# Score tiles in runs of six, whole turns and hashes, whole v products, and three two-bank score buffers

One NeuronCore of one Trainium2 chip. The metric is the device time of one execution in microseconds, the median over several runs; lower is better.

## The reference

Hash attention feeds a feed-forward block. Queries and keys get a six-bit hash; a query sees only keys of its own bucket. The result goes through two matrices with a PReLU between.

```python
batch, n_heads, seq, head_dim = (4, 8, 768, 64)          # proj: (64, 6)
q_bucket, k_bucket = ...                                  # sign bits of q @ proj, k @ proj
scores = np.where(q_bucket == k_bucket, q @ k.T / 8, -1e9)
x = softmax(scores) @ v                                   # -> (3072, 512)
h = x @ w_in                                              # w_in (512, 2048)
g = np.maximum(h, 0) + alpha * np.minimum(h, 0)
out = g @ w_out                                           # w_out (2048, 512)
```

## The kernel before

Heads are worked on in 16 pairs, each in two units of 384 queries. For a unit there are six score tiles (128 keys by two heads by 384 queries), each a bf16 hash product plus a float32 product in one two-bank buffer of PSUM (the memory in which this kernel's TensorE products land; it uses eight banks of it), followed by one exp on ScalarE (ACT). A "turn" is the transposition of q or k. Probabilities are multiplied with v on TensorE (PE) and added up on VectorE (DVE), one addition being done by an accumulating DMA. Meanwhile DVE prepares the feed-forward weights, so that each feed-forward block needs seven products instead of eight. Each block has three accumulators in PSUM, called a, b and c. Early in the feed-forward a "verdict" is reached: a check of the largest magnitudes, which says whether the result of this fast way may stand.

```python
psum = tc.tile_pool(name="ps", bufs=2, space=PSUM)        # tags sc (2 banks each), mi, av: 8 banks

def turn(pi, name, half):            # 3 transposes into one "mi" bank, one ACT copy
def hash_bits(pi, half):             # 4 matmuls into one "mi" bank, three ACT signs
def scores(u, part):                 # two score tiles
    for kc in (2 * part, 2 * part + 1):
        sc = psum.tile([P, 2, 512], F32, tag="sc")
        ...                          # 4 matmuls, then exp on ACT into pt
def attend(u, half): ...             # v product over 3 key tiles into "av"
def totals(u): ...                   # sum over keys into "mi"

class Product:                       # one feed-forward block
    def times(self, bank, left, right, start):
        if start:
            tag, shape = {"a": ("sc", [P, 2, 512]), "b": ("mi", [P, 512]), "c": ("av", [P, 512])}[bank]
            t = psum.tile(shape, F32, name=f"{self.name}{bank}", tag=tag)
            self.ps[bank] = (t[:, 0] if bank == "a" else t)[:, : self.width]
        ...
    # 1: a, ACT copies a; 2: b; 22: DVE adds b; 5: c, ACT copies c; 6: a, ACT copies a;
    # 3: c, DVE adds c; 7: a, ACT copies a; 4 (after step 1 of the next block): a

for u in range(UNITS):               # shortened: order of the TensorE work
    scores(u, 0)
    turn(pi + 1, "q", ...) or hash_bits(pi + 1, 0)
    attend(u - 1, 0)
    scores(u, 1)
    attend(u - 1, 1); totals(u - 1)
    scores(u, 2)
    turn(pi + 1, "k", ...) or hash_bits(pi + 1, 1)
```

## Time and profile before

| | before |
|---|---|
| time, median of the 3 runs (range) | 975.83 us (975.73 to 978.42) |
| PE busy, share of the span | 98% |
| attention, first score to first product b of the feed-forward | 12.7 to 386.0 us |
| feed-forward, from there to the end | 386 to 973 us |
| one pair of heads in attention | 23.15 us |
| one feed-forward block, first matrix / second matrix | 9.03 / 24.17 us |

A row of waits is: who waited <- for whom: us in total, times, longest. A row of busy time is: stretch, length, then busy time of PE, weight loads, DVE, ACT and POOL with counts, granted clock of PE (1.00 is full speed), DMA share, GB/s. A timeline row is: start, length, engine, source line, operation, tiles written and read, part of the array in use with shape and type, count, and in brackets the idle time before it with what ended it.

### The profile page before, as it was taken

The numbers are of one execution on the slowest core, as the hardware profiler recorded it, in microseconds if no ns is written. First come the engines' busy times: TensorE is split into PE (matmuls) and PEld (weight loads), VectorE is DVE, ScalarE is ACT, GpSimd is POOL, SyncE is SP. The second block draws the span as 40 slices with busy tenths as digits, with TensorE's granted clock in tenths as the row PEclk, the third lists the DMA queues.
The fourth block names the chain that finished last, engine by engine and source line by source line (L and its number), as shares of the span: only waits on it lengthen the run. The fifth ranks groups of instructions, "written<-read, shape, count | busy, mean of one in ns | idle before, by whom it ended". The sixth has DMA issues, their size and how long they took to land.

```text
span 973.3 us, 12433 instructions
## 1 busy us (share of the span) xinstructions
PE 953.9 (98%) x4741; PEld 589.9 (61%) x4741; DVE 552.9 (57%) x995; ACT 371.5 (38%) x669; POOL 64.8 (7%) x62
## 2 busy tenths in 40 slices
PE   6999999999999999999999999999999999999997
PEld 3444444444444444556888556888556888556885
DVE  3788888898998887765400665301666301666000
ACT  6777776777777773222000222001222001222000
POOL 1000110000000010000300000200001200000000
PEclk9999999999999999999999999999999999999999
DMA  8767879699777643844100234100234100221000
GB/s 208 166 157 174 217 175 291 164 224 225 193 198 193 161 125 88 347 190 140 49 23 33 76 113 143 47 24 31 76 114 154 47 22 22 87 103 38 22 22 25
DMA packets 102020, 119.40 MB, mean 123 GB/s; under 512 B 53808, under 2 KB 88640, under 8 KB 101952
## 3 DMA queue, kind: packets, MB, share of 16 engines
q1 hardware_dynamic: 91680, 105.54, 34.7%
q0 software_dynamic: 8704, 12.58, 7.6%
q8 instruction: 39, 0.64, 0.3%
q10 hardware_dynamic: 1568, 0.39, 0.2%
q14 instruction: 29, 0.24, 0.1%
HBM read 78.65 MB, written 27.26 MB: 109 GB/s over the span
## 4 chain that ended last, share of the span: by engine, by line
PE 97%; ACT 1%; DVE 1%; DMA 0%; issue 0%; SPq 0%; ACTq 0%; DVEq 0%
PE sc L668 16%; PE av L703 14%; PE z_2a L773 6%; PE z_1a L773 6%; PE z_0a L773 6%; PE z_2c L773 3%; PE z_1c L773 3%; PE z_0c L773 3%; PE hs L651 2%; PE f_0a L773 2%; PE sm L715 2%; PE f_2a L773 2%; PE f_3a L773 2%; PE f_7a L773 2%; PE f_6a L773 2%; PE f_5a L773 2%
## 5 line engine op out<-in xcount | busy, mean ns | idle before, releaser
L673 ACT ACTIVATE pt<-sc 128x768 f32<-128x768 f32 x192 | 150.3, 813 | 97.4 <-PE sc L668 92.6
L668 PE MATMUL sc<-qT,kT 64*128 64x384 f32 x768 | 155.2, 482 | 0.0
L703 PE MATMUL av<-pt,vn 128*64 128x385 f32 (+1 forms) x768 | 138.1, 495 | 0.0
L703 PEld LDWEIGHTS av<-pt,vn 128*64 128x64 f32 x768 | 49.4, 136 | 76.7 <-issue 76.7
L827 DVE TENSOR_TENSOR g<-g,g 128x384 f32<-128x384 f32 x128 | 84.0, 677 | 2.2
L668 PEld LDWEIGHTS sc<-qT,kT 64*128 64x128 f32 x768 | 68.7, 189 | 21.0 <-issue 20.9
L668 PE MATMUL sc<-qb,kb 64*128 64x384 bf16 x384 | 63.6, 328 | 2.7 <-ACT pt L673 2.6
L685 POOL DMA_DIRECT2D accp<-pt x32 | 38.5, 1204 | 335.0 <-ACT pt L673 161.3
L668 PEld LDWEIGHTS <-kb 64*128 64x128 bf16 x384 | 19.1, 93 | 66.1 <-issue 52.3
L773 PE MATMUL z_2a<-wo,g 128*128 128x256 f32 x256 | 58.0, 379 | 0.5 <-ACT z_2u L780 0.5
L773 PE MATMUL z_0a<-wo,g 128*128 128x256 f32 x256 | 57.9, 379 | 0.0
L773 PE MATMUL z_1a<-wo,g 128*128 128x256 f32 x256 | 57.9, 379 | 0.0
L773 PEld LDWEIGHTS z_2a<-wo,g 128*128 128x128 f32 x256 | 48.6, 190 | 8.1 <-ACT z_2u L780 0.9
L773 PEld LDWEIGHTS z_0a<-wo,g 128*128 128x128 f32 x256 | 48.6, 190 | 7.5
L773 PEld LDWEIGHTS z_1a<-wo,g 128*128 128x128 f32 x256 | 48.6, 190 | 6.6
L820 DVE SCALAR_TENSOR_TENSOR g<-h,alpha 128x384 f32<-128x384 f32 x32 | 20.8, 652 | 50.5 <-ACT h L812 50.5
L749 POOL TENSOR_TENSOR x<-x,x 128x768 f32<-128x768 f32 x12 | 23.9, 2000 | 359.4 <-DMA x<-x_s 358.9
L654 ACT ACTIVATE qb<-hs,hb 32x384 bf16<-32x384 f32 x64 | 36.7, 573 | 2.3 <-PE hs L651 1.1
L690 DVE TENSOR_TENSOR accd<-accd,pt 128x768 f32<-128x768 f32 x32 | 30.7, 959 | 4.1 <-ACT kT L630 1.0
L693 DVE TENSOR_TENSOR accd<-accd,accp 128x768 f32<-128x768 f32 x32 | 30.5, 952 | 3.1 <-DMA accp<-pt 3.1
L689 DVE TENSOR_TENSOR accd<-pt,pt 128x768 f32<-128x768 f32 x32 | 30.4, 949 | 0.5 <-ACT pt L673 0.5
L682 DVE TENSOR_TENSOR accp<-pt,pt 128x768 f32<-128x768 f32 x32 | 30.5, 952 | 0.0
(218 smaller groups left out, 1443.5 us busy)
## 6 DMA issues: line engine op xcount, KB each, us to landing
wi<-w_in_s SPq DMA_DIRECT2D x32, 896.0 KB, 4.6
accp<-pt POOLq DMA_DIRECT2D x32, 384.0 KB, 7.2
raw<-in_moe_w_in_dram SPq DMA_DIRECT2D x16, 512.0 KB, 4.8
raw<-in_moe_w_out_dram SPq DMA_DIRECT2D x16, 512.0 KB, 4.4
w_in_s<-wsi SPq DMA_DIRECT2D x16, 448.0 KB, 6.8
w_out_s<-wso SPq DMA_DIRECT2D x8, 896.0 KB, 7.5
wo<-w_out_s SPq DMA_DIRECT2D x8, 896.0 KB, 8.4
qn<-in_q_dram SPq DMA_DIRECT2D x32, 192.0 KB, 3.7
```

The costliest lines, as they stand in the source:

```text
L654: do(ACT.activation(bits["q", pi][D * s : D * s + 32, cols], ps[r], AF.Sign, bias=hb[r]))
L668: do(PE.matmul(sc[:, s, :CW], what["k", pi][r, ks], what["q", pi][r, qs], start=first, stop=not first,))
L673: do(ACT.activation(pt[:, :, :CW], sc[:, :, :CW], AF.Exp, scale=SCALE / DOWN))
L682: do(DVE.tensor_tensor(accp[u], p(u, 0), p(u, 1), op=ALU.add))
L685: nc.gpsimd.dma_start(accp[u], p(u, 2), accum_op=ALU.add)
L689: do(DVE.tensor_tensor(accd[u], p(u, 3), p(u, 4), op=ALU.add))
L690: do(DVE.tensor_tensor(accd[u], accd[u], p(u, 5), op=ALU.add))
L693: do(DVE.tensor_tensor(accd[u], accd[u], accp[u], op=ALU.add))
L703: do(PE.matmul(av[u][D * s : D * s + D, :w], nat["v", pi][:, s, kc * D : (kc + 1) * D], prob[u, kc][:, s, :w], start=(kc == 0), stop=(kc = ...
L749: do(engine.tensor_tensor(x_m[b, to], x_m[b, a], x_m[b, c], op=ALU.subtract))
L773: do(PE.matmul(self.ps[bank], self.left(left, k), self.right(right, k), start=start and k == 0, stop=k == self.nk - 1, skip_group_check=no ...
L827: do(DVE.tensor_tensor(g_m[to, i], g_m[x, i], g_m[y, i], op=op))
```

## The change

The intent: PE never idles in attention once it is under way, but loses about 0.1 us each time the shape of the array changes. So do more of one kind in a row. A unit becomes one run of six score tiles (three of this unit, three of the next), one run of hashes or turns, one v product with the sum inside. A run of six needs three score buffers of two banks; that leaves two banks, so b and the sums share one buffer "sm", "av" gets one, and the feed-forward's c moves into the second bank of a's score buffer.

```diff
-    psum = ... tc.tile_pool(name="ps", bufs=2, ...)
+    psum = ... tc.tile_pool(name="ps", bufs=1, ...)
+    def two_banks(name):
+        return psum.tile([P, 2, 512], F32, name=name, tag="sc", bufs=3)
-    def turn(pi, name, half):        # and hash_bits(pi, half): half the columns each
+    def turn(pi, name):              # all 768 columns, in a score buffer; so hash_bits(pi)
...
-    def scores(u, part):             # two tiles
+    def scores(u, half):             # three tiles
...
-                tag, shape = {"a": ("sc", [P, 2, 512]), "b": ("mi", [P, 512]), "c": ("av", [P, 512])}[bank]
-                t = psum.tile(shape, F32, name=f"{self.name}{bank}", tag=tag)
-                self.ps[bank] = (t[:, 0] if bank == "a" else t)[:, : self.width]
+                if bank == "a":
+                    self.both = two_banks(f"{self.name}a")
+                t = psum.tile([P, 512], F32, name=f"{self.name}b", tag="sm") if bank == "b" else self.both[:, "ac".index(bank)]
+                self.ps[bank] = t[:, : self.width]
...
+    scores(0, 0); add_first(0); turn(1, "q"); turn(1, "k"); weight_abs(0)
+    for pi in range(2): ...          # four magnitudes of q and k on ScalarE
     for u in range(UNITS):
+        scores(u, 1); scores(u + 1, 0)
+        hash_bits(pi + 1) or turn(pi + 2, "q"), turn(pi + 2, "k")
+        attend(u, 0); totals(u); attend(u, 1)
...
-        for st in ((2, 22, 6, 3, 7) if j == 0 else (2, 22, 5, 6, 3, 7)):
+        for st in ((6, 3, 7, 2, 22) if j == 0 else (2, 22, 5, 6, 3, 7)):
```

(The final verdict's four transposes also go into one bank with one reduction.)

More of the change, by code (lines that the diff above doesn't have):

```diff
@@ L443, in fast_path @@
     mid = ctx.enter_context(tc.tile_pool(name="mid", bufs=2))
-    psum = ctx.enter_context(tc.tile_pool(name="ps", bufs=2, space=bass.MemoryType.PSUM))
+    psum = ctx.enter_context(tc.tile_pool(name="ps", bufs=1, space=bass.MemoryType.PSUM))
     attn = ctx.enter_context(ExitStack())
@@ L509, in setup_alpha @@
     def setup_alpha():
-        ps = psum.tile([P, NF], F32, name="alps", tag="mi")
+        ps = psum.tile([P, NF], F32, name="alps", tag="sm")
         do(PE.transpose(ps, alpha16, ident[:NF, :NF]))
@@ L620, in weight_sums @@
             fn(*x)
-    def turn(pi, name, half):
+    def two_banks(name):
+        return psum.tile([P, 2, 512], F32, name=name, tag="sc", bufs=3)
+    def turn(pi, name):
         src = nat[name, pi].rearrange("p c h d -> p c (h d)")
-        if half == 0:
-            tr[name, pi] = pool.tile([P, S], F32, name=f"{name}T{pi}", tag=f"{name}T")
-        ps = psum.tile([P, CW], F32, name=f"tp_{name}{pi}{half}", tag="mi")
-        for i in range(CH):
-            do(PE.transpose(ps[:, i * P : (i + 1) * P], src[:, CH * half + i], ident))
+        tr[name, pi] = pool.tile([P, S], F32, name=f"{name}T{pi}", tag=f"{name}T")
+        ps = two_banks(f"tp_{name}{pi}")
+        for c in range(NC):
+            do(PE.transpose(ps[:, c // CH, c % CH * P :][:, :P], src[:, c], ident))
         do(ACT.activation(
-            tr[name, pi][:, half * CW : (half + 1) * CW], ps, AF.Copy, scale=DOWN if name == "q" else 1.0,
+            tr[name, pi].rearrange("p (h w) -> p h w", h=2), ps[:, :, :CW], AF.Copy,
+            scale=DOWN if name == "q" else 1.0,
         ))
@@ L638, in magnitude, with hash_bits, sign @@
         do(ACT.activation(t, t, AF.Square, accum_out=mags[:, n, pi : pi + 1]))
-    def hash_bits(pi, half):
-        if half == 0:
-            bits["q", pi] = qbs[pi % 2]
-            bits["k", pi] = pool.tile([P, S], BF16, name=f"kb{pi}", tag="kb")
-        cols = slice(half * CW, (half + 1) * CW)
-        ps = psum.tile([P, CW], F32, name=f"hs{pi}{half}", tag="mi")
-        for s in range(2):
-            for n, name in enumerate("kq"):
-                r = D * s + 32 * n
-                do(PE.matmul(ps[r : r + 32], wh[s], tr[name, pi][:, cols], start=True, stop=True))
-        for s in range(2):
-            r = slice(D * s + 32, D * s + D)
-            do(ACT.activation(bits["q", pi][D * s : D * s + 32, cols], ps[r], AF.Sign, bias=hb[r]))
-        do(ACT.activation(bits["k", pi][:, cols], ps, AF.Sign, bias=hb))
-    def scores(u, part):
+    def hash_bits(pi):
+        bits["q", pi] = qbs[pi % 2]
+        bits["k", pi] = pool.tile([P, S], BF16, name=f"kb{pi}", tag="kb")
+        ps = two_banks(f"hs{pi}")
+        for half in range(2):
+            for s in range(2):
+                for n, name in enumerate("kq"):
+                    r = D * s + 32 * n
+                    do(PE.matmul(
+                        ps[r : r + 32, half, :CW], wh[s], tr[name, pi][:, half * CW : (half + 1) * CW],
+                        start=True, stop=True,
+                    ))
+        def sign(t, rows, ps_rows):
+            do(ACT.activation(
+                t[rows].rearrange("p (h w) -> p h w", h=2), ps[ps_rows, :, :CW], AF.Sign, bias=hb[ps_rows],
+            ))
+        for s in range(2):
+            sign(bits["q", pi], slice(D * s, D * s + 32), slice(D * s + 32, D * s + D))
+        sign(bits["k", pi], slice(0, P), slice(0, P))
+    def scores(u, half):
         pi, g = divmod(u, NCH)
         qs = slice(g * CW, (g + 1) * CW)
-        for kc in (2 * part, 2 * part + 1):
-            sc = psum.tile([P, 2, 512], F32, name=f"sc{u}_{kc}", tag="sc")
+        for kc in range(half * NC // 2, (half + 1) * NC // 2):
+            sc = two_banks(f"sc{u}_{kc}")
             ks = slice(kc * P, (kc + 1) * P)
@@ L682, in add_first @@
         do(DVE.tensor_tensor(accp[u], p(u, 0), p(u, 1), op=ALU.add))
-    def add_third(u):
         nc.gpsimd.dma_start(accp[u], p(u, 2), accum_op=ALU.add)
@@ L712, in totals @@
     def totals(u):
-        sums[u] = psum.tile([P, CW], F32, name=f"sm{u}", tag="mi")
+        sums[u] = psum.tile([P, CW], F32, name=f"sm{u}", tag="sm")
         for s in range(2):
@@ L858, in verdict @@
         do(DVE.tensor_reduce(top[:, 3:4], alpha, axis=mybir.AxisListType.X, op=ALU.max))
+        ps = psum.tile([1, 4, P], F32, name="vd", tag="av")
         for n in range(4):
-            ps = psum.tile([1, P], F32, name=f"vd{n}", tag="mi")
-            do(PE.transpose(ps, top[:, n : n + 1], ident))
-            do(DVE.tensor_reduce(row[:, n : n + 1], ps, axis=mybir.AxisListType.X, op=ALU.max))
+            do(PE.transpose(ps[:, n], top[:, n : n + 1], ident))
+        do(DVE.tensor_reduce(row, ps, axis=mybir.AxisListType.X, op=ALU.max))
         do(DVE.tensor_tensor(row[:, 0:1], row[:, 0:1], row[:, 1:2], op=ALU.mult))
@@ L870, in verdict @@
         do(DVE.tensor_scalar(flag, row[:, 0:1], -1.0, 1.0, op0=ALU.mult, op1=ALU.add))
+    last = UNITS - 1
     load(0, "q")
@@ L877, in fast_path @@
     for name in "qk":
-        for half in range(2):
-            turn(0, name, half)
-    for half in range(2):
-        hash_bits(0, half)
+        turn(0, name)
+    hash_bits(0)
     setup_alpha()
@@ L884, in fast_path @@
     load(1, "k")
-    load(1, "v")
     for i in range(3):
         load_weight(i)
+    load(1, "v")
+    scores(0, 0)
+    add_first(0)
+    for name in "qk":
+        turn(1, name)
+    weight_abs(0)
+    for pi in range(2):
+        for name in "qk":
+            magnitude(pi, name)
+            load(pi + 2, name)
     for u in range(UNITS):
         pi, g = divmod(u, NCH)
-        more = pi + 1 < NPAIR
-        scores(u, 0)
-        if u == 0:
-            weight_abs(0)
-            magnitude(0, "q")
-            magnitude(0, "k")
-        if u > 0:
-            add_last(u - 1)
-        weight_parts(u)
-        if u > 0:
-            add_total(u - 1)
-        add_first(u)
-        if more:
-            if g == 0:
-                turn(pi + 1, "q", 0)
-                turn(pi + 1, "q", 1)
-            else:
-                hash_bits(pi + 1, 0)
-        if u > 0:
-            attend(u - 1, 0)
-        scores(u, 1)
-        add_third(u)
+        scores(u, 1)
+        if u < last:
+            scores(u + 1, 0)
+        add_last(u)
+        add_total(u)
+        if u < last:
+            add_first(u + 1)
+        else:
+            now = ff1(0, 0)
+            now.step(1)
+            now.step(5)
+        if g == 0 and pi + 1 < NPAIR:
+            hash_bits(pi + 1)
+        if g == 1 and pi + 2 < NPAIR:
+            turn(pi + 2, "q")
+            turn(pi + 2, "k")
+        weight_parts(u)
+        attend(u, 0)
+        totals(u)
         weight_sum(u)
@@ L914, in fast_path @@
         weight_group(u)
-        if u > 0:
-            attend(u - 1, 1)
-            totals(u - 1)
-            if g == 0 and 0 < pi < NPAIR - 1:
-                load(pi + 1, "v")
-        scores(u, 2)
-        if u > 0:
-            divide(u - 1)
-        if more:
-            if g == 0:
-                turn(pi + 1, "k", 0)
-                turn(pi + 1, "k", 1)
-            else:
-                hash_bits(pi + 1, 1)
+        attend(u, 1)
+        if u == last:
+            weight_sums(4)
+        divide(u)
+        if g == 1 and pi + 2 < NPAIR:
+            load(pi + 2, "v")
         load_weight(u + 3)
@@ L937, in fast_path @@
             weight_abs(u + 1)
-        if more:
-            magnitude(pi + 1, "qk"[g])
-            if pi + 2 < NPAIR:
-                load(pi + 2, "qk"[g])
-    late = []
-    last = UNITS - 1
-    now = ff1(0, 0)
-    attend(last, 0)
-    now.step(1)
-    add_last(last)
-    add_total(last)
-    attend(last, 1)
-    now.step(5)
-    totals(last)
-    divide(last)
-    weight_sums(4)
+        p2, name = pi + 1 + g, "kq"[g]
+        if 2 <= p2 < NPAIR:
+            magnitude(p2, name)
+            if p2 + 2 < NPAIR:
+                load(p2 + 2, name)
+    late = []
     attn.close()
```

## The prediction

> **What bounds the kernel now.** I read the page first. TensorE (PE) is busy 98% of the span and heads the chain that ended last; VectorE (DVE) is at 57% and ScalarE (ACT) at 39% over the whole, because the second part of the kernel uses them little.
>
> ```profile
> PE 953.9 (98%) x4741; PEld 589.9 (61%) x4741; DVE 552.9 (57%) x995; ACT 371.5 (38%) x669; POOL 64.8 (7%) x62
> PE 97%; ACT 1%; DVE 1%; DMA 0%; issue 0%; SPq 0%; ACTq 0%; DVEq 0%
> ```
>
> Next the waits of PE, to see whether anything but PE's own work can be removed. They add up to 12.6 us, all at the start or near 410 us:
>
> ```profile
> PE tp_q L629 <- DMA qn<-in_q_dram: 6.1, 1, 6.1
> PE sc L668 <- ACT pt L673: 2.6, 2, 2.4
> PE vd L861 <- DVE top L856: 2.0, 1, 2.0
> PE alps L511 <- ACT kb L656: 1.1, 1, 1.1
> ```
>
> Then the busy time by window over the attention part. PE has not one idle moment in 300 us, but its neighbours are not far off: DVE 263.37 of 300, ACT 219.23.
>
> ```profile
> 60.00:360.00 300.00, 300.00 (x2026) 131.33 (x2022) 263.37 (x471) 219.23 (x363) 31.20 (x26) 1.00 0.77 197
> ```
>
> So a gain must come out of the PE stream itself. The timeline of PE shows it, start to start:
>
> ```profile
> 204.57 0.34 PE L668 MATMUL sc<-qb,kb 64*128 64x384 bf16 x2
> 204.75 0.81 PE L668 MATMUL sc<-qT,kT 64*128 64x384 f32 x4
> 205.39 0.33 PE L668 MATMUL sc<-qb,kb 64*128 64x384 bf16 x2
> 205.56 0.81 PE L668 MATMUL sc<-qT,kT 64*128 64x384 f32 x4
> 206.29 0.87 PE L629 MATMUL tp_k<-ident,kn 128*128 128x128 f32 x6
> 207.10 0.34 PE L668 MATMUL sc<-qb,kb 64*128 64x384 bf16 x2
> ...
> 209.60 2.16 PE L703 MATMUL av<-pt,vn 128*64 128x385 f32 x12
> 211.69 0.34 PE L668 MATMUL sc<-qb,kb 64*128 64x384 bf16 x2
> ...
> 213.41 2.16 PE L703 MATMUL av<-pt,vn 128*64 128x385 f32 x12
> 215.41 0.81 PE L715 MATMUL sm<-accd,ones 128*64 128x384 f32 x4
> 216.15 0.34 PE L668 MATMUL sc<-qb,kb 64*128 64x384 bf16 x2
> ...
> 227.72 0.34 PE L668 MATMUL sc<-qb,kb 64*128 64x384 bf16 x2
> ```
>
> The shape after the engine is the part of the array in use: 64*128 for scores, 128*64 for v products and sums, 128*32 for hashes, 128*128 for turns. Four float32 score matmuls take 0.64 us when another score tile follows (204.75 to 205.39), but 0.73 when a turn follows (205.56 to 206.29). The v product takes 2.09 when scores follow and 2.00 when the sum, of the same shape, follows. Every change of shape costs about 0.1 us, though PE counts as busy. One pair of heads runs from 204.57 to 227.72, 23.15 us, and this period repeats without variation.
>
> **What the Trainium skill says.** "TensorEngine Tiling (Array Packing)", section Tiling Modes, Key Properties: "Changing tiling mode (not just tile) drains the TensorE". The trace agrees and gives the size, 0.10 us to leave plus 0.01 to 0.06 to enter. "Perfetto Trace Analysis", section Identifying the Most-Contended Engine, warns that matmul busy share is a poor measure because matmuls are pipelined; indeed PE is 100% busy here while drains recur. "PSUM — Partial Sum Buffer", section Specifications, gives 8 banks: before they are two score buffers of two, two "mi" and two "av"; after, three of two, one "sm" and one "av", 8 both times. "TensorE: Matmul & The Clock Gate", Part 1, halves the clock after an idle window of about 3.4 us; no steady stretch here is idle, but the start may be.
>
> **The change, part by part: shape changes.** Before, a pair (two units of 384 queries) has six score runs S of two tiles, four runs X (turn q, turn k, two half hashes), and four v products A, two of them with the sum: 14 boundaries. After, a unit is one S of six tiles, one X (a whole hash in one unit, both turns in the other), one A with the sum inside: 6 boundaries a pair. From start-to-start times of single matmuls in the same trace (mean over 30 to 360 us):
> - S: the last score matmul takes 413 ns instead of 319 at the end of a run, the first bf16 pair 170 instead of 160. 0.104 us a run; four runs fewer: 0.416.
> - A: entry 368 instead of about 316 (0.052), exit 416 to 419 instead of 316 (0.10). Before four entries and four exits, after two of each: 0.304.
> - Turns: entry 164 instead of 109, exit 205 instead of 109: 0.15 saved once a pair.
> - Hashes: a run of 8 takes 0.78, of which two groups of four work at 0.323 each; the remaining 0.13 is saved once.
> Sum 0.416 + 0.304 + 0.15 + 0.13 = **1.00 us a pair**, so the period should go from 23.15 to 22.15. Fifteen full pairs give 14.9 us. The last pair has no X and saves some 0.5, and at the end of attention two separate feed-forward products sit side by side, 0.3 more. Together 15.7 us of PE work.
>
> **Does PE still find everything ready?** Let T be the start of a run of six. A tile takes PE 0.81 (204.57 to 205.39). ACT's exp takes 0.81 from start to end, but starts follow each other at 0.69 when the tiles are ready, so with three buffers tile n needs only exp n-3, done about 0.6 us earlier. The run ends at T+4.95. X takes 1.43 to 1.46, half the v product 1.0, so the sum is wanted at T+7.4. DVE can begin its adds at T+2.6 (second exp) and does three at 1.05, 0.88 and 0.87: done at T+5.4, 2 us early. "av" has one buffer; its last read by the division comes some 2 us into the next unit, and it is wanted at T+6.3. The accumulating DMA takes 7.2 us (median) and has about 9.
>
> The load: DVE's 263.37 of 300 us is 10.16 a unit (300 us hold 25.9 units of 11.575); 11.08 will be left, 92%. ACT's is 8.5, or 76%. Wider turns and signs only save ACT instructions. PE remains the bound, but DVE has under 1 us a unit to spare.
>
> **Edges.** Start: before, PE waits 6.1 + 1.1 + 2.4. After, the signs take whole 768 columns. One of 384 takes 0.573, and going by exp over 768 at 0.812 against a copy over 384 at 0.50, one of 768 should take 0.89; three in a row follow the hashes, so scores start at about 14.4 instead of 12.7. Then four magnitudes (0.83 each) stand on ACT ahead of the second run's exps: 3.4 us of PE wait. I carry PE work forward to unit 1 and get its first score at 31.0. Before, PE had at 30.98 done one score tile more and 8 hash matmuls fewer, nearly the same. Net loss 0 to 2, taken as 0.5.
>
> End: the last three units have no X, or little, so PE needs 9.6 us where DVE needs about 10.4: a stall of some 0.7 in the sums. Bank "b" of the feed-forward has one buffer instead of two. In the first block its reader, a DVE add, now comes behind two others that wait for memory of the attention part (before, DVE sat 3.6 us until 394.25). I estimate 1.8 of PE wait, once. Verdict: four transposes in a row and one reduce instead of a ping-pong saves 0.35. From there to the end PE runs one shape without waits, 550 us that stay.
>
> Sum: 975.8 - 15.7 + 0.5 + 0.7 + 1.8 - 0.35 = **962.8 us**, 1.3% faster.
>
> **Rivals.**
> (1) DVE becomes the bound. At 92% a late accumulating DMA or the four extra subtractions in the middle (0.87 each) could delay the sums. For it: two windows of 30 us in that stretch already have DVE at 27.4 and 28.0. Against: 2 us of slack before each sum. If true the period stays at 22.5 to 22.8 and the time is 967 to 971.
> (2) The six-tile run waits for ACT, as the second chunk of the first unit does now (2.4 us for exp). For it: the hash and turns use the same three buffers, and late signs or magnitudes would delay the first exps. Against: ACT's other work ends by about T+10.5 of 11.1, and exps run faster than tiles. A wait of 0.3 a unit would eat 9 us: 972.
> (3) Ends decide: single-buffered "b" stalls in every block instead of once, or both banks of a shared buffer are treated as one, so that each copy blocks the next product (about 0.5 in each of 44 blocks): 985. Against: separate banks can be tracked apart, and in steady state DVE reads "b" many microseconds before it is due.
> (4) More gain than counted, if fewer drains also remove losses inside runs. Little room: inside runs the trace already shows 323 ns for each 384 columns, everywhere. At most 958.
>
> **Range and chances.** The 1.00 a pair is measured from the same instructions and I trust it within 0.1, which is 1.5 us; the ends add about 3 either way, and rivals 1 and 2 pull upwards. Range 957.5 to 969. Over 2% needs below 956.3, more than all drains removed would give even with free ends: 6%. Within 2%: 91%. Slower by over 2% only through rival 3 in a worse form: 3%.
>
> **What would show it.** Right: the changed PE timeline has score runs of 12 rows, about 4.95 us from first score to X; the period is 22.1 to 22.2; PE busy is 100% over 60 to 340 with no waits in it; ACT's signs and turns are half as many; attention ends about 14 us earlier and the feed-forward is as long as before. Wrong: PE waits for ACT exps or DVE sums in every unit, a period over 22.4, leaving a shape still costing 0.1 but a gain of half; or waits on "b" beyond the first block.

## The result

The changed kernel takes **1083.27 us** (1081.14 to 1084.06, 4 runs) against 975.87 (the three runs above and one more): ratio 1.109 (95% interval 1.1066 to 1.1114). It is 11% slower; the prediction said 1.3% faster. A ratio is always the mean time of one kernel's fast runs over the mean of the other's fast runs of the same rounds, so it is not quite the ratio of the medians.

The page of the changed kernel, its engine line and the chain that ended last:

```profile
PE 979.2 (91%) x4741; PEld 591.9 (55%) x4741; DVE 553.1 (51%) x992; ACT 363.8 (34%) x589; POOL 64.0 (6%) x62
PE 89%; ACT 5%; DVE 4%; issue 1%; DMA 0%; DVEq 0%; SPq 0%; ACTq 0%
```

The same 4741 matmuls, but PE is idle for 9% of the span, and ACT and DVE have entered the chain. The busy time over the attention part shows that it is not lost there:

```profile
60.00:340.00 280.00, 280.00 (x1976) 137.13 (x1974) 258.42 (x459) 207.71 (x290) 30.00 (x25) 1.00 0.80 204
```

PE has no idle moment; DVE is at 92.3% and ACT at 74%, where 92 and 76 were predicted. The PE timeline of one unit:

```profile
60.27 0.34 PE L678 MATMUL sc<-qb,kb 64*128 64x384 bf16 x2
...
65.22 0.87 PE L631 MATMUL tp_q<-ident,qn 128*128 128x128 f32 x6
65.94 0.82 PE L631 MATMUL tp_k<-ident,kn 128*128 128x128 f32 x6
66.68 2.16 PE L711 MATMUL av<-pt,vn 128*64 128x384 f32 x12
68.67 0.81 PE L723 MATMUL sm<-accd,ones 128*64 128x384 f32 x4
69.31 2.10 PE L711 MATMUL av<-pt,vn 128*64 128x384 f32 x12
71.35 0.34 PE L678 MATMUL sc<-qb,kb 64*128 64x384 bf16 x2
```

A run of six takes 4.95 us (60.27 to 65.22), as predicted, and a unit 11.08. Two units take 22.13 us against 23.15: 1.02 us a pair saved, predicted 1.00.

What is lost lies after attention. Some of the waits of PE (there are 38 such lines, one for each kind of wait):

```profile
PE f_2a L782 <- DVE f_2u L824: 2.9, 4, 0.7
PE f_2a L782 <- ACT f_2p L789: 2.3, 4, 0.6
PE f_2a L782 <- ACT f_2u L789: 2.3, 4, 0.6
PE sc L678 <- ACT kb L659: 2.6, 1, 2.6
PE sc L678 <- ACT pt L683: 3.0, 1, 3.0
```

The first three repeat for every block of the feed-forward. Four products of a block before the change (c, a, c, a: steps 5, 6, 3, 7), then four after (a, c, a: steps 6, 3, 7, and the next block's first a):

```profile
434.33 1.45 PE L773 MATMUL f_5c<-x,wi 128*128 128x384 f32 x4
435.62 1.45 PE L773 MATMUL f_5a<-x,wi 128*128 128x384 f32 x4
436.91 1.45 PE L773 MATMUL f_5c<-x,wi 128*128 128x384 f32 x4
438.20 1.45 PE L773 MATMUL f_5a<-x,wi 128*128 128x384 f32 x4
```
```profile
582.45 1.56 PE L782 MATMUL f_2a<-x,wi 128*128 128x384 f32 x4 [0.57 <-ACT f_2p L789]
584.57 1.56 PE L782 MATMUL f_2a<-x,wi 128*128 128x384 f32 x4 [0.57 <-ACT f_2u L789]
586.85 1.56 PE L782 MATMUL f_2a<-x,wi 128*128 128x384 f32 x4 [0.72 <-DVE f_2u L824]
588.24 1.45 PE L782 MATMUL f_3a<-x,wi 128*128 128x384 f32 x4
```

Before, products follow each other every 1.29 us. After, both accumulators bear the name of the tile that they share ("f_2a"), and three times a block a product waits until the reader of the *other* accumulator is done: a for the copy of c (f_2p), c for the copy of a (f_2u), a for the addition that reads c. (What ended a wait is read from semaphore events: the waiting product waits for a semaphore that the copy or the addition raises.) A block of the first matrix takes 11.69 us instead of 9.03, one of the second 26.48 instead of 24.17. From the first product b to the last, 43 blocks later, the kernel before takes 558.9 us and the changed one 665.4: 106.5 us lost. The first block's products ahead of its b and the last block after its b lie outside these marks and lose some 6.6 more: about 113 in all.

Each wait costs more than its bracket shows. The brackets of a block sum to 1.86 us, the block loses 2.66: 0.27 more for each wait. A product is listed with 1.45 us but normally overlaps the next by 0.16, and that overlap is gone; the first product after a wait takes 1.39 to the next start instead of 1.29.

The start is slower too. Score tiles of the first two runs:

```profile
22.25 0.34 PE L678 MATMUL sc<-qb,kb 64*128 64x384 bf16 x2
23.07 0.33 PE L678 MATMUL sc<-qb,kb 64*128 64x384 bf16 x2
...
27.82 0.47 PE L678 MATMUL sc<-qb,kb 64*128 64x384 bf16 x2 [2.96 <-ACT pt L683]
29.32 0.56 PE L678 MATMUL sc<-qb,kb 64*128 64x384 bf16 x2
```

Tiles follow at 0.82 us before a wait of 2.96 us and at 1.5 to 1.6 us after it. From 15.66 us on, after a wait of 2.64, they took 1.6 us too. The clock granted to PE goes with it (the number before the last two):

```profile
25.00:30.00 5.00, 2.19 (x10) 1.47 (x11) 1.39 (x2) 4.57 (x10) 0.00 (x0) 0.79 1.01 207
```

The 0.79 is a mean: the trace lists half clock from 27.9 to 31.3 us, which is the stretch of slow tiles. Its first clock record begins at 21.07 us, where the earlier slow tiles end; before that the view prints 1.00 for want of a record, which is no measurement. The first score of unit 1 comes at 38.1 us, where the prediction had 31.0.

### The profile page after: what moved, and what is told of

Read it like the earlier page. It is cut to its first block, busy times and chain, and to the rows that moved or that the text cites. A ratio compares the mean times of both kernels' runs of the same rounds, so it can differ in the third digit from the quotient of the medians.

```text
span 1081.4 us, 12297 instructions
## 1 busy us (share of the span) xinstructions
PE 979.2 (91%) x4741; PEld 591.9 (55%) x4741; DVE 553.1 (51%) x992; ACT 363.8 (34%) x589; POOL 64.0 (6%) x62
## 4 chain that ended last, share of the span: by engine, by line
PE 89%; ACT 5%; DVE 4%; issue 1%; DMA 0%; DVEq 0%; SPq 0%; ACTq 0%
PE sc L678 14%; PE av L711 11%; PE z_2a L782 8%; PE z_1a L782 8%; PE z_0a L782 8%; PE f_2a L782 3%; PE f_3a L782 3%; PE f_1a L782 3%; PE f_7a L782 3%; PE f_5a L782 3%; PE f_4a L782 3%; PE f_6a L782 3%; PE f_0a L782 3%; PE hs L653 2%; PE sm L723 2%
## 5 line engine op out<-in xcount | busy, mean ns | idle before, releaser
L782 PE MATMUL z_2a<-wo,g 128*128 128x256 f32 x384 | 88.2, 383 | 6.9 <-ACT z_2u L789 2.5
L782 PE MATMUL z_0a<-wo,g 128*128 128x256 f32 x384 | 88.0, 382 | 6.0 <-DVE o L853 2.3
L782 PE MATMUL z_1a<-wo,g 128*128 128x256 f32 x384 | 88.0, 382 | 6.0 <-DVE o L853 2.3
L782 PEld LDWEIGHTS z_0a<-wo,g 128*128 128x128 f32 x384 | 72.0, 190 | 21.0 <-DVE o L853 3.9
L782 PEld LDWEIGHTS z_1a<-wo,g 128*128 128x128 f32 x384 | 72.0, 190 | 20.1 <-DVE o L853 3.9
L782 PE MATMUL f_0a<-x,wi 128*128 128x384 f32 x96 | 36.3, 500 | 9.6 <-DVE f_0u L824 4.5
L782 PE MATMUL f_2a<-x,wi 128*128 128x384 f32 x96 | 37.3, 512 | 7.4 <-DVE f_2u L824 2.9
L782 PE MATMUL f_3a<-x,wi 128*128 128x384 f32 x96 | 36.7, 506 | 7.4 <-DVE f_3u L824 2.9
L782 PE MATMUL f_7a<-x,wi 128*128 128x384 f32 x96 | 36.1, 499 | 7.8 <-DVE f_7u L824 3.2
L782 PE MATMUL f_1a<-x,wi 128*128 128x384 f32 x96 | 36.1, 499 | 7.7 <-DVE f_1u L824 2.9
```

Of the source, the lines that this page charges most:

```text
L782: do(PE.matmul(self.ps[bank], self.left(left, k), self.right(right, k), start=start and k == 0, stop=k == self.nk - 1, skip_group_check=no ...
```

## The experiments

Ten runs of nine kernels, all with right results. Theory A: in the feed-forward, two accumulators in one tile make PE wait for readers of the other. Rivals: the single buffer of b, too few buffers in all, or the attention order.

**two_tiles: the changed kernel, c in a tile of its own.** Everything else is kept, c's place in a second bank too.

```diff
-                if bank == "a":
-                    self.both = two_banks(f"{self.name}a")
-                t = psum.tile(..., tag="sm") if bank == "b" else self.both[:, "ac".index(bank)]
+                if bank == "b":
+                    t = psum.tile([P, 512], F32, name=f"{self.name}b", tag="sm")
+                else:
+                    t = two_banks(f"{self.name}{bank}")[:, "ac".index(bank)]
```

> The changed kernel, with the products a and c of a feed-forward block in two tiles (c in the second bank of a tile of its own) instead of two banks of one tile. Everything else stays, the single buffer of b too. Theory A (two banks in one tile make PE wait for the reader of the other bank, three times a block): blocks go back from 11.69 and 26.48 us to 9.03 and 24.17, so 1083 falls by 114 to 116 to about 968. Rival B (the single buffer of b, or too few buffers in all): waits stay, time over 1050. Rival C (attention part lost it): time stays near 1083.

970.68 us (968.80 to 972.18), before on the same chip 977.33, ratio 0.9935 (0.9908 to 0.9961). The waits are gone; two products of one block in PE's timeline:

```profile
427.96 1.45 PE L783 MATMUL f_5c<-x,wi 128*128 128x384 f32 x4
429.25 1.45 PE L783 MATMUL f_5a<-x,wi 128*128 128x384 f32 x4
```

One declaration is worth about 113 us (112.6 between medians on two chips, whose kernels before differ by 1.5). b still has a single buffer, and waits once, 2.3 us, in the second block. Theory A stands; rivals B and C fall as the main cause. Buffers were not what was short: a block here takes two of the three score buffers, where the changed kernel took one.

**before_shared: the kernel before, with only the shared tile.**

```diff
-                tag, shape = {"a": ("sc", [P, 2, 512]), "b": ("mi", [P, 512]), "c": ("av", [P, 512])}[bank]
-                t = psum.tile(shape, F32, name=f"{self.name}{bank}", tag=tag)
-                self.ps[bank] = (t[:, 0] if bank == "a" else t)[:, : self.width]
+                if bank == "a":
+                    self.both = psum.tile([P, 2, 512], F32, name=f"{self.name}a", tag="sc")
+                t = psum.tile(..., tag="mi") if bank == "b" else self.both[:, "ac".index(bank)]
+                self.ps[bank] = t[:, : self.width]
```

> The kernel before, with one thing of the change: products a and c of a block take the two banks of one score buffer; b keeps two buffers, attention is untouched. Theory A: attention ends as before (PE at 386 us at the first product b), every block is 2.3 to 2.7 us longer, in all 1088 to 1093. Rival B: no change, 976.

1096.35 us (1095.27 to 1097.50), ratio 1.122. The cause alone gives the whole loss, without any other part of the change. It is 3 us over the expected range; one wait in the first block is 4.4 us long.

**flat_tile: the changed kernel, the shared tile declared as 1024 columns.**

```diff
-                    self.both = two_banks(f"{self.name}a")
+                    self.both = psum.tile([P, 1024], F32, name=f"{self.name}a", tag="sc", bufs=3)
-                ... self.both[:, "ac".index(bank)]
+                ... self.both[:, 512 * "ac".index(bank) :][:, :512]
```

> The changed kernel with the shared buffer declared flat, 1024 columns, a in columns 0 to 383 and c in 512 to 895. If the waits come from how the two-dimensional tile is sliced they vanish: 970. If any two parts of one tile are ordered where a reader stands between, they stay: 1083.

1079.84 us in a single run, with the same waits (again 2.9 us in total for the additions of most blocks). So it is the common tile and not the way it is sliced. Two disjoint bank-wide parts of one tile are put in order by the program's own semaphores; right results did not need that order, as two_tiles gives them without it. (Where the two banks lie to each other was not varied by itself.)

**before_whole_v: the kernel before, with only the whole v product.**

```diff
-        if u > 0:
-            attend(u - 1, 0)
         scores(u, 1)
...
         if u > 0:
+            attend(u - 1, 0)
             attend(u - 1, 1)
             totals(u - 1)
```

> The kernel before, with one other thing of the change alone: both halves of the v product and the sum in one run, in the place of the second half. A unit then has one entry to (0.052) and one exit from (0.100) the shape of the v product less: 0.152 us a unit, 4.9 us for 31 or 32 units, 971.0. If the drains were not what costs, the time stays at 976; if the later v product makes PE wait, it grows.

1006.39 us (1005.61 to 1009.43), ratio 1.029: a miss. PE's wait for exp, which was 2.6 us in all, is now, in the view of its waits:

```profile
PE sc L668 <- ACT pt L673: 33.7, 31, 2.4
```

977.3 - 4.9 + (33.7 - 2.6) gives 1003.5; the remaining 2.9 would be 0.09 for each of 31 waits, overlap lost as in the feed-forward, which is argued and not measured. So this run doesn't test the price of a drain. The half v product stood between two score runs, and its 2 us were ACT's time to empty the two score buffers. Taking the boundary away took that time too. The expectation named this outcome but did not work it out.

**two_score_buffers: the changed order with two score buffers.** Banks as before, c in "av".

```diff
-        return psum.tile([P, 2, 512], F32, name=name, tag="sc", bufs=3)
+        return psum.tile([P, 2, 512], F32, name=name, tag="sc", bufs=2)
-    psum = ... bufs=1
+    psum = ... bufs=2                                     # sm and av twice
+                tag={"b": "sm", "c": "av"}[bank]          # and a alone in its score buffer
```

> The changed order, with banks as in the kernel before: two score buffers of two banks, two one-bank buffers for sums and b, two for v products and c. Buffer theory: from the third tile on, a tile waits for the exp of the one two before it, some 0.2 us a tile with the exps at 0.81 us and a tile at 0.81, and hashes and turns wait too: 1 to 2 us a unit, 32 to 60 us, in all 1000 to 1030, PE below 95% busy. Rival: the third buffer does nothing (ACT is quick enough) and it runs at 965 to 972; with b in two buffers the 2.3 us wait at the first blocks goes.

995.95 us (995.50 to 996.46), ratio 1.020, a little under the expected range. In the timeline the third and the fifth tile of a run wait:

```profile
210.26 0.34 PE L678 MATMUL sc<-qb,kb 64*128 64x384 bf16 x2 [0.17 <-ACT pt L683]
...
212.21 0.34 PE L678 MATMUL sc<-qb,kb 64*128 64x384 bf16 x2 [0.15 <-ACT pt L683]
```

A pair takes 24.02 us instead of 22.13. The third buffer, which is why c had to move, is worth 25 us in this order (970.7 on another chip against 996.0; the chips' kernels before differ by 1.3). Only two tiles in a run pay, not each one, 0.33 us each from start to start, and the turn or hash after them shares the rest, so the cost of about 0.95 us a unit is just under the expected 1 to 2.

**split_run: two_tiles with the run of six cut in two by hashes or turns.**

```diff
         scores(u, 1)
-        if u < last:
-            scores(u + 1, 0)
...
             turn(pi + 2, "k")
+        if u < last:
+            scores(u + 1, 0)
         weight_parts(u)
+        if u < last:
+            add_first(u + 1)
```

> two_tiles with the run of six score tiles cut in two of three by the hashes or turns, which adds one score run a unit and nothing else (the first addition for the next unit moves behind the weight parts on VectorE, because its inputs come later). Drain theory: 0.104 us a unit, period of a pair 22.14 to 22.35, in all 3.3 us slower than two_tiles. Rival: the order makes PE wait for exps or sums, as moving the v product did; then waits show in every unit and it costs more than 10 us.

1003.77 us (1001.23 to 1006.50), ratio 1.028. The rival's outcome, a second miss of the same kind. PE's waits:

```profile
PE sc L678 <- ACT kb L659: 19.0, 16, 2.6
PE sm L723 <- DVE accd L701: 9.6, 10, 3.0
```

With hashes in the middle, the signs stand on ACT in front of exps whose buffers PE wants. Among the first twelve units, from sum to sum, those with hashes take 12.44 us where two_tiles has 11.05. The units with turns have no wait; they take 11.19, where two_tiles has 11.08: one score run more costs 0.11, expected 0.104. So the drain has its predicted price, and the order's effect on ACT is many times larger. The waits for sums begin only at 191 us; whether they come from later exps or from the addition that this edit also moved on DVE was not tried.

**warm: two_tiles with idle transposes in the two waits at the start.**

```diff
+    def keep_warm(n, count):
+        ps = psum.tile([P, P], F32, name=f"warm{n}", tag="sm")
+        for _ in range(count):
+            do(PE.transpose(ps, ident, ident))
     setup_alpha()
+    keep_warm(0, 14)
...                                   # and keep_warm(1, 26) after scores(0, 1)
```

> As two_tiles, with idle transposes on PE in the two waits at the start (14 after the first hashes, 26 between the third and fourth score tile of the first unit), results thrown away. Theory W: after each of these waits of 2.6 and 3.0 us score tiles run at 1.60 us instead of 0.81 because PE was idle, so with the idle gone they run at 0.81 and the kernel is 3 to 4.5 us faster than two_tiles. Rival: the slow tiles come from something else at the start (DMA load, first use), and the time stays or grows by up to 1 us.

966.34 us (965.32 to 966.97), ratio 0.9883, against 970.68 in the same rounds: 4.3 us for work that computes nothing. After the transposes, tiles come at 0.81 us at once:

```profile
13.90 2.75 PE L889 MATMUL warm<-ident 128*128 128x128 f32 x14 [0.27 <-DVE alpha L512]
16.59 0.34 PE L678 MATMUL sc<-qb,kb 64*128 64x384 bf16 x2
17.40 0.33 PE L678 MATMUL sc<-qb,kb 64*128 64x384 bf16 x2
```

Theory W is shown in part. In the profiled run of two_tiles (969.22 us) the tiles after the first wait were slow (1.6 us, then 1.4), those after the second, 2.97 us, were not. Against the profiled run of warm (966.97 us) it is 1.05 us later, from the first sum over keys to the last. Another 1.69 us lie at 404 to 409 us, far from the start: both kernels wait 2.06 us there for the verdict, but after it two_tiles is listed at half clock for 3.4 us and two products take 2.14 us instead of 1.29, while warm keeps its clock. So not all of the 4.3 us need come from the transposes. The two runs of two_tiles near 972 us list a mean clock of 0.995, the two near 969 us 0.997; that more stretches of half clock are what spreads its times over 3.4 us is likely, but not shown.

**short_start: two_tiles with a start of its own.**

```diff
-    turn(0, "q"); turn(0, "k"); hash_bits(0)
+    first_turn("q", 0); first_turn("k", 0); first_turn("q", 1); first_turn("k", 1)   # halves
+    first_hash(0); first_hash(1)
-    four magnitudes before unit 0, loads after them
+    load(2, "q"); load(2, "k")       # q and k get three input buffers; one magnitude a unit
```

> two_tiles with a start of its own: first turns and hashes in halves, in single banks; the four magnitudes out of ScalarE's way (one a unit, three input buffers for q and k instead of two). The score run of unit 1 then starts at 27 to 30 us instead of 38, and the kernel is at 959 to 962, below warm at 966. If the slow tiles remain it stays over 966.

960.31 us (959.34 to 961.02), ratio 0.9838; again as **short_start_2**: 959.74, ratio 0.9828 (0.9815 to 0.9842). The first score of unit 1 comes at 28.3 us. Of the 9.3 us between the profiled runs of two_tiles and short_start, 7.5 are gained before the first sum over keys, and 1.7 are the stretch of half clock at 404 us, which short_start does not have. The parts of the new start were not run apart.

> The same kernel as short_start again, as the pair of short_both_ends on the same chip: 960.3 within 1.

**short_both_ends: two waits after attention taken away as well.** The seam is where attention gives way to the feed-forward.

```diff
+                if bank == "b" and self.name == "f0_0":
+                    t = two_banks(f"{self.name}b")[:, 0]
-        for st in ((6, 3, 7, 2, 22) if j == 0 else ...
+        for st in ((2, 22, 6, 3, 7, 4) if j == 0 else ...
+        if j == 2:
+            verdict_tops()           # the verdict's reductions, ahead of the block's additions
```

> short_start with two waits at the seam taken away: product b of the first block goes into the third score buffer and the block's additions come in the order 11, 12, 22, 21 (so the second block's b need not wait for them, 2.3 us), and the reductions for the verdict come a block earlier (2.1 us). Against it, the second block's a must wait for one copy, about 0.9. Expected 3 to 3.7 us below short_start: 956.5 to 957.5, 1.9 to 2.0% faster than before. If VectorE's wait for the attention part's memory is what binds there, the wait moves to another product and the gain is under 1.5.

955.67 us (955.16 to 955.93), ratio **0.9784** (0.9771 to 0.9797), faster than both kernels; 4.1 us below short_start in the same rounds, a little over the expected 3 to 3.7. PE's two longest waits that are left:

```profile
PE tp_q L899 <- DMA qn<-in_q_dram: 6.8, 1, 6.8
PE sc L678 <- ACT kb L917: 1.1, 1, 1.1
```

## Why the prediction was wrong

- **Shape changes, 1.00 us a pair**: right. 1.02 measured, in a stretch without waits.
- **PE finds everything ready in attention**: right, with three score buffers. DVE's share came out at 92.3% for 92. Rivals 1 and 2 did not happen. two_score_buffers and split_run show how near rival 2 was.
- **"From there to the end PE runs one shape without waits, 550 us that stay": this is the step that failed.** The text named the mechanism under rival 3, "both banks of a shared buffer are treated as one, so that each copy blocks the next product", and put it aside with "separate banks can be tracked apart". It also mis-sized it, "about 0.5 in each of 44 blocks". The runs show three waits a block, 0.45 to 0.72 us visible and about 0.27 hidden each, 2.66 or 2.31 us a block, 113 us in all. The skill's page on PSUM, which I had cited for the number of banks, doesn't tell which semaphores the program is given. Whether the order is drawn by tile or by bank was open, and the diff put two accumulators with readers in turn into one tile; that should have carried far more weight than 3%.
- **Start, net 0.5**: wrong in size. The first score of unit 1 was put at 31.0 us and came at 38.1. The hashes stayed slow throughout (0.64 us a group), so scores began at 15.7 and not 14.4; the slow tiles cost 2.4 and about 1.7; and half a v product was taken as 1.0 us although the shown row has 2.0. The working of the 31.0 is not shown; if it used that 1.0, the first whole v product with its sum, 4.7 us in the trace, came out some 2 short, and the four together, less 0.4 for a wait of 3.0 instead of 3.4, make up about 7.1. The clock was cited in the text as a risk and then not priced. The slip about half a v product also put the sum's deadline at T+7.4 instead of T+8.4, with no effect.
- **End**: right in size. The wait for b was 2.3 us for 1.8, the sum waited 0.4 for 0.7 (both in two_tiles).
- Slips without effect: ACT's share is 38%, not 39%, and one of the waits before (0.5 us) lies at 963 us, not at the start or near 410.

With the failed step mended the prediction would have been near: two_tiles takes 970.7 us, 969.2 in its profiled run, against 962.8. In that run the first score of unit 1 comes at 35.8, 4.8 later than predicted with 0.5 allowed for, and the kernel before is 1.5 us slower on that chip: together 5.8 of the 6.4. (Smaller terms, among them 1.7 for the half clock at 404 us, differ in both directions.)

## What to carry to other kernels

When buffers are merged to make room, look at who reads each part and when: two accumulators with alternating writers and readers need tiles of their own, even where their banks are apart. When PE is busy without a gap, count drains by start-to-start times, but check what each boundary gives the other engines: a piece of PE work between two runs can be the time in which ACT empties the buffers. A wait of 2 to 3 us on PE cost 1.7 to 2.4 us more in slow matmuls behind it in some runs and nothing in others, so a start is worth laying out by hand, and a gain of 1 to 2 us worth a look at the listed clock.

## What the Trainium skill lacked or had wrong

- No page says that two banks of one PSUM tile may be ordered against each other by the generated program. "PSUM — Partial Sum Buffer", section PSUM bank collisions raise a hardware error, asks for order only within a bank and quadrant; here one shared tile cost about 113 us, and separate tiles ran without these waits.
- "TensorEngine Tiling (Array Packing)", section Tiling Modes, Key Properties, says that a change of mode drains the engine but gives no size: here 0.10 us to leave and 0.01 to 0.06 to enter; 0.11 measured for one score run more.
- "TensorE: Matmul & The Clock Gate", Part 1, puts the fall back to half clock after an idle window of about 3.4 us, of windows that run freely. The length of one wait does not decide it here: half clock was listed for 3.4 us after a wait of 2.96 in the changed kernel (tiles from 0.82 to 1.6 us) and not after 2.97 in two_tiles, and after 2.06 in two_tiles and not after 2.06 in warm. Freely running windows would fit that; no run tests it.
- "Perfetto Trace Analysis", section Identifying the Most-Contended Engine, warns that matmul busy share misleads. The runs add that idle brackets do too: 1.86 us shown in a block that lost 2.66.
